# The tail of a one-core transformer block in another order: all of W1 for the first half of the last block before the last exp, the first part of Wo taken forward, and a second g buffer

## The chip, the core and the metric

The kernel runs on one core of a Trainium2 chip. A core has a matrix engine (TensorE, PE in the profile; PEld are its weight loads), a vector engine (VectorE, DVE), a scalar engine for table functions (ScalarE, ACT), a general engine (GpSimd, POOL) and a queue that issues transfers (SyncE, SP). Each works through its own list of instructions in order and waits on semaphores for the others. The metric is the device time of one execution in microseconds; three timed executions of the kernel before gave 780.62, 780.99 (the median) and 781.88.

## The reference

One transformer block with adaptive layer norm, on x of 2048 tokens by 512 channels, 32 heads of 16 channels, and a hidden layer of 1376:

```
mod = (silu(c) @ w_mod) split in six: sa, ca, ga, sb, cb, gb
h   = layernorm(x) * (1 + ca) + sa
q, k, v = h @ wqkv, per head
p   = softmax(q k^T * Dh ** -0.5)
x   = x + ga * ((p v) @ wo)
h   = layernorm(x) * (1 + cb) + sb
out = x + gb * (gelu(h @ w1 + b1) @ w2 + b2)
```

Weights and activations are bfloat16, sums are float32, GELU is the tanh form.

## The kernel before

**Tiling.** Queries are cut into 4 blocks of 512 tokens (`QB`), keys into 16 tiles of 128. A run is one query block with 4 heads, whose channels lie in four groups of 32 rows; there are 32 runs. In the last block a run holds 8 heads and 256 queries instead (`run_heads`), so that after half of its runs the first 256 of the last 512 tokens are complete. One unit is a score product of one head group with one key tile: a 32-row matmul of 512 columns (L803).

**Exps.** Scores go to PSUM tiles of three and two banks in turn (`st`, one buffer each), and ACT takes the exp of a whole tile (L852, `pt`). Some key tiles (`DKS`, 4 of 16) are done by DVE instead: scores in a one-bank tile (`ax`, two buffers) are turned into the bits of an approximate exponential (L900), and four shifted copies of them (L932, L953 on DVE; parts of the last one, L938, on POOL) are summed by the product with V. L994 is that product, on four column groups at once; it also sums the denominators.

**After a run** (`normalise`) DVE copies the result (L1019); SP moves the denominators through DRAM in small transfers (L1025, L1027), DVE takes their reciprocal (L1030), SP brings them back as a full tile (L1035, L1040), POOL multiplies (L1046) and SP moves rows to their place (L1056).

**After a block** (`block_tail`): the product with Wo (L1151), the sum with x (L1200), layer norm (`layer_norm`, statistics on DVE, the inverse root as an addition and a power on POOL, L604 and L606), transposes on PE (L672) and the scale and shift (`modulate`, L618 on DVE, L615 on ACT), W1 (L1217), the addition of b1 while leaving PSUM (L1227), one GELU over the block (L1236, with a table load before and after it), W2 (L1157), the last sum (L1248), and the transfer out. Wo and W2 hold the gates ga and gb, multiplied in by POOL early (L1069). In the last block `block_tail` runs for its first 256 tokens (`part`): W1 of the first 8 of 11 groups f of 128 hidden channels goes through DVE before the last exp, the other three (`direct`) after it, from the score banks that have come free (`r_t`, tiles `t`), with GELU straight from PSUM (L1223).

**The last 256 tokens** (`last_half`) are two tiles, t = 2 and 3. For each: transpose, reciprocal, transpose back and product on DVE (L1283, L1285, L1287, L1290), the two parts of Wo (L1151, L1297), sum (L1301), statistics, power, z (L610), transposes (L1317), modulation, W1 (L1329), GELU (L1332), W2, last sum (L1344).

**Order.** All engines' lists are written by a planner in the kernel (`Plan`), which runs through the operations with assumed durations and latencies. At each step it picks on each engine the ready operation with the lowest value of `dyn` (for PE) or `prio`, with a random scatter whose seed comes from `SEEDS`, one for each 12.5 us of planned time. `due` spreads a block's tail over a number of units (`TAIL`, `TAIL2`, `TAIL3`); kinds in `urgent` get 0.5, a second score tile in advance 2.2, P·V 3.0. The plan keeps a count of recent PE activity (`done`), and where this is low it puts in warming products on zeros (L430, L446, `heat`). The modulation columns (`mod_mm`, L575) are products of one output column, with a warming product after each second group (L578).

The lines that the planned order hangs on, in `dyn`:

```
        if o.kind == "qkA":
            back = n_a[0] - n_a[1]
            return (0.0 if back == 0 else 2.2 if back == 1 else 6.0) + same
...
        if o.kind in urgent:
            return 0.5 + same
        if o.kind == "last":
            return o.prio + 0.1 * same
```

## Time and profile before

| what | value |
|---|---|
| median of three timed executions | 780.99 us |
| the profiled execution, its own time | 779.58 us |
| its span, first to last instruction | 777.8 us |
| ACT busy | 750.5 us (96%) |
| PE busy | 722.0 us (93%) |
| DVE busy | 712.7 us (92%) |
| POOL busy | 281.2 us (36%) |
| mean granted TensorE clock | 0.995 |
| end of the last exp | 754.84 us |

The profile is that of one execution, and its span is shorter than its time by what lies around the program. A busy share is an average over stages: nearly all of the span is the attention, in which ACT is hardly ever idle, and the last 23 us are the tail of the last 256 tokens, in which it is idle half of the time. What counts for the end is therefore when ACT gets through its exps, and how long the chain behind the last one takes. Rows of a timeline give the start in the span, the duration, engine, line and operation, the tile written and read, and how often in a row; in brackets the idle time before it and what ended this.

### The profile page before, as it was taken

What the parts mean: (1) busy time and instruction counts of PE and PEld (TensorE: products, weight loads), DVE (VectorE), ACT (ScalarE), POOL (GpSimd) and SP (SyncE); (2) the same over time, 40 slices, a digit from 0 to 9 for tenths busy, and PEclk for the clock granted to TensorE, in tenths of its full rate; (3) what the DMA queues carried; (4) which work ended last, traced back from release to release, by engine and by line L of the source; (5) the groups of instructions that cost most, each with busy time, mean ns of one, the idle gap of its engine ahead of it and who ended that gap; (6) DMA issues with size and microseconds to landing.
All of it is one profiled execution on the core that took longest, in us unless ns stands there. A gap on an engine that the chain in (4) does not pass through costs nothing.

```text
span 777.8 us, 20624 instructions
## 1 busy us (share of the span) xinstructions
PE 722.0 (93%) x8233; PEld 274.2 (35%) x8307; DVE 712.7 (92%) x1180; ACT 750.5 (96%) x680; POOL 281.2 (36%) x622
## 2 busy tenths in 40 slices
PE   8888999999999889999998999999999999989998
PEld 3433333233333232323332323223234444434455
DVE  6777999999899999999999989999989998999964
ACT  3999999999999999999999999999999999999994
POOL 5221433444533334454444433333322423233320
PEclk9999998999999999999999999999999999999999
DMA  7033011000011010000100010000111000100010
GB/s 217 28 107 124 16 27 43 12 24 13 22 43 54 23 47 23 19 6 22 44 20 21 15 35 16 26 23 16 39 48 29 22 22 16 46 25 18 25 46 28
DMA packets 39074, 28.23 MB, mean 36 GB/s; under 512 B 17957, under 2 KB 34374, under 8 KB 38978
## 3 DMA queue, kind: packets, MB, share of 16 engines
q1 hardware_dynamic: 38970, 26.91, 12.1%
q8 instruction: 65, 1.06, 0.6%
q14 instruction: 31, 0.25, 0.1%
q10 hardware_dynamic: 8, 0.00, 0.0%
HBM read 21.30 MB, written 2.61 MB: 31 GB/s over the span
## 4 chain that ended last, share of the span: by engine, by line
ACT 50%; PE 27%; DVE 12%; issue 9%; DMA 1%; POOL 0%; SPq 0%; ACTq 0%; DVEq 0%; POOLq 0%
ACT pt L852 46%; PE od L994 9%; PE st L803 8%; DVE ph L900 5%; PE ax L1157 3%; DVE sh L953 2%; ACT g L1236 2%; PE ax L803 2%; DVE ph L953 1%; PE ax L693 1%; DMA blk<-in_w_mod_dram 1%; DVE sl L932 1%; DVE g L1227 1%; PE ax L1217 1%; PE t L1157 1%
## 5 line engine op out<-in xcount | busy, mean ns | idle before, releaser
L852 ACT ACTIVATE pt<-st 128x1536 bf16<-128x1536 f32 x626 | 708.6, 1408 | 4.4 <-PE st L803 2.3
L900 DVE TENSOR_SCALAR ph<-ax 128x512 int16<-128x512 f32 x484 | 318.1, 682 | 25.2 <-PE ax L803 22.3
L938 POOL TENSOR_TENSOR sl<-ph,step 128x128 int32<-128x128 int32 x358 | 163.7, 459 | 327.3 <-DVE sh L953 105.3
L803 PE MATMUL st<-qm,kT 32*128 32x512 bf16 x1564 | 245.7, 384 | 32.5 <-ACT pt L852 25.0
L803 PEld LDWEIGHTS <-kT 32*128 32x128 bf16 x2048 | 86.6, 91 | 244.1 <-issue 232.5
L803 PE MATMUL ax<-qm,kT 32*128 32x512 bf16 x484 | 162.5, 381 | 3.5 <-DVE ph L900 2.8
L994 PEld LDWEIGHTS <-VEB 128*32 128x32 bf16 x4992 | 109.6, 96 | 150.2 <-issue 128.0
L994 PE MATMUL od<-pt,VEB 128*32 128x512 bf16 (+1 forms) x1952 | 150.8, 344 | 0.9 <-ACT pt L852 0.5
L953 DVE TENSOR_SCALAR sh<-ph 128x4096 int16<-128x4096 int16 x121 | 146.9, 1217 | 2.5 <-PE od L994 2.2
L994 PE MATMUL od<-ph,VEB 128*32 128x512 bf16 (+1 forms) x1216 | 90.1, 340 | 1.7 <-DVE OD L1019 1.0
L994 PE MATMUL od<-sh,VEB 128*32 128x512 bf16 (+1 forms) x1216 | 84.6, 340 | 1.6 <-DVE sh L953 0.8
L953 DVE TENSOR_SCALAR ph<-ph 128x2048 int16<-128x2048 int16 x121 | 83.0, 687 | 0.4
L932 DVE TENSOR_SCALAR sl<-ph 128x1024 int16<-128x1024 int16 (+3 forms) x121 | 57.7, 482 | 0.4 <-PE od L994 0.4
L1046 POOL TENSOR_TENSOR OT<-OD,RB 128x128 bf16<-128x128 f32 x76 | 35.4, 470 | 48.1 <-DVE sh L953 14.8
L994 PE MATMUL od<-sl,VEB 128*32 128x512 bf16 (+1 forms) x608 | 48.4, 342 | 0.3
L1217 PE MATMUL ax<-blk,W 128*128 128x512 bf16 (+1 forms) x142 | 39.2, 358 | 2.0 <-issue 0.8
L1046 POOL TENSOR_TENSOR OS<-OD,RB 128x128 bf16<-128x128 f32 x48 | 22.8, 476 | 39.4 <-DVE sl L932 15.6
L693 PE MATMUL ax<-blk,w 128*128 128x512 bf16 x100 | 33.4, 383 | 3.3 <-ACT blk L615 1.7
L1227 DVE TENSOR_SCALAR g<-ax,b1c 128x512 bf16<-128x512 f32 (+1 forms) x41 | 28.0, 691 | 3.9 <-PE ax L1217 3.0
L1157 PE MATMUL ax<-w,g 128*128 128x512 bf16 x101 | 28.9, 381 | 1.1 <-DVE ph L900 0.6
L599 DVE BATCH_NORM_STATS2 ln_s<-xb 128x6 f32<-128x512 bf16 x32 | 21.6, 676 | 1.4 <-DMA xb<-in_A_x_dram 1.3
L1157 PEld LDWEIGHTS <-g 128*128 128x128 bf16 x176 | 13.7, 97 | 22.5 <-issue 12.8
(112 smaller groups left out, 400.8 us busy)
## 6 DMA issues: line engine op xcount, KB each, us to landing
RB<-rn SPq DMA_DIRECT2D x124, 64.0 KB
xb<-in_A_x_dram SPq DMA_DIRECT2D x8, 512.0 KB
out_dram<-o SPq DMA_DIRECT2D x16, 128.0 KB
qm<-qs SPq DMA_DIRECT2D x120, 16.0 KB
W<-in_B_w_dram SPq DMA_DIRECT2D x1, 1376.0 KB
w<-in_A_wqkv_dram SPq DMA_DIRECT2D x3, 384.0 KB
blk<-in_w_mod_dram SPq DMA_DIRECT2D x2, 512.0 KB
g<-in_w_mod_dram SPq DMA_DIRECT2D x2, 512.0 KB
```

The source lines that it names most:

```text
L693: return chain([(lambda ps, j=j: nc.tensor.matmul(out=ps[:, 0:QB], lhsT=w.tile[:, j, cc * P:(cc + 1) * P], rhs=o_h[b].tile[:, j, :], start ...
L803: nc.tensor.matmul(out=o.tile[:, k * QB:(k + 1) * QB], lhsT=kT[cc][kb][rows, ko * P:(ko + 1) * P], rhs=qm.tile[rows, par, :] if hb is None ...
L852: nc.scalar.activation(out=e.tile[:, 0:len(got) * QB], in_=o.tile[:, 0:len(got) * QB], func=ACT.Exp, scale=ESC)
L900: nc.vector.tensor_scalar(out=ph.tile[:, c0:c0 + QB], in0=o.tile, scalar1=PH_B, scalar2=0.0, op0=ALU.add, op1=ALU.max)
L932: parts = [in_turn(op("DVE", lambda o: nc.vector.tensor_scalar(out=into.tile[:, 0:cols], in0=first.tile[:, 0:cols], scalar1=PH_SH[-1], sca ...
L938: after_dve(nc.gpsimd.tensor_tensor(out=into.tile[:, c].bitcast(I32), in0=first.tile[:, c].bitcast(I32), in1=step, op=ALU.add))
L953: o = op("DVE", lambda o: nc.vector.tensor_scalar(out=dst(o), in0=src(), scalar1=PH_SH[j], scalar2=None, op0=ALU.add), us, deps, lat=DL, p ...
L994: nc.tensor.matmul(out=o_od[r].tile[32 * i:32 * i + 32, n * HB:n * HB + w], lhsT=v_tile(kt)[:, c0:c0 + 32], rhs=got[i][:, at:at + w], star ...
L1046: two = beside(lambda c: nc.gpsimd.tensor_tensor(out=OT.tile[:, c], in0=OD.tile[:, c], in1=o5.tile[:, c], op=ALU.mult), (OT,), (OD, o5))
L1157: nc.tensor.matmul(out=ps, lhsT=g[:, f, col:col + P], rhs=rhs, start=(f == 0), stop=(f == NF - 1))
L1217: mm = chain([(lambda ps, f=f, j=j: nc.tensor.matmul(out=ps[:, 0:N], lhsT=W1[:, j, f * P:(f + 1) * P], rhs=h.tile[:, j, 0:N], start=(j == ...
L1227: ev.append(op("DVE", lambda o, f=f, mm=mm: nc.vector.tensor_scalar(out=g.tile[:, f, 0:N], in0=mm.tile[:, 0:N], scalar1=b1c[:, f:f + 1], s ...
```

## The change

The first 256 tokens of the last block get a g buffer of their own (`r_gp`), so that all 11 groups of W1 go through DVE into it before the last exp, and the `direct` way through the score banks goes. GELU over that buffer is cut in four (`GE`) and comes after the last exp as before. The kind of this work becomes `late`, which is in `urgent`. The new buffer also holds the two broadcast gates until they are multiplied into the weights, in place of two constant tiles. `early_wo` takes the load of x for the last tiles and the first three products of Wo out of `last_half`; it is called when the next to last run has ended. In `last_half` the two tiles have a transposed buffer each, the second tile's DVE chain has other priorities and gates, the addition of EPS moves from POOL to DVE (L1316 of the changed kernel), and the transposes of tile 3 use the `ax` banks. W2 of the first half uses `r_t` banks, and its last sums wait for the second tile's z. The plan counts the modulation columns with less PE activity (`act`). `TAIL2` and `TAIL3` get smaller, and all values of `SEEDS` but the first are other ones (that line is left out below).

```diff
...
-        self.kb, self.due, self.extra = 0, 1e9, False
+        self.kb, self.due, self.extra, self.act = 0, 1e9, False, None
...
-            self.done.append((s, (o.us if o.mode[0] != "qk" else o.us * (len(o.mode) - 1) / 4)))
+            self.done.append((s, o.act if o.act is not None else (o.us if o.mode[0] != "qk" else o.us * (len(o.mode) - 1) / 4)))
...
+    LD = 0.11
...
-    PSUM_F = 8
...
+    r_gp = res("gp", 1, [P, NF, QB // 2], BF16)
...
-    urgent = set()
+    urgent = {"late"}
...
-            return (2.5 if o.due + 16 > prog() else 0.8) + same
+            return (2.5 if o.due + 16 > prog() else 0.8 if o.due + 48 > prog() else 0.3) + same
...
     TAIL, CB = 185, 49
-    TAIL2, TAIL3 = 148, 95
+    TAIL2, TAIL3 = 100, 60
     plan = Plan(dyn, later)
...
-        for n, (fn, us) in enumerate(pieces):
+        for n, (fn, us, *act) in enumerate(pieces):
...
+            o.act = act[0] if act else None
...
-    ga_bc = const.tile([P, D], FP32, name="ga_bc")
-    gb_bc = const.tile([P, D], FP32, name="gb_bc")
...
     def mod_columns(dst, ws, kind, warmer=True):
-        mm = chain([(lambda ps, n=n, w=w, m=m: mod_mm(ps, n, w[1](), m, warmer), 0.36 if warmer else 0.22)
+        mm = chain([(lambda ps, n=n, w=w, m=m: mod_mm(ps, n, w[1](), m, warmer), 0.36 if warmer else 0.22, 0.17 * (m % 2) + 0.01)
                     for n, w in enumerate(ws) for m in range(NC)],
...
             got += beside(lambda c, w=w: nc.gpsimd.tensor_tensor(
-                out=w()[:, c], in0=w()[:, c], in1=gate_t[:, c], op=ALU.mult), deps, prio=2.0)
+                out=w()[:, c], in0=w()[:, c], in1=gate_t()[:, c], op=ALU.mult), deps, prio=2.0, rel=(o_late["gates"],))
         return op("NIL", None, 0.0, got, lat=0.0, prio=0.0)
+
+    def gate_tile(n):
+        return lambda: o_late["gates"].tile.rearrange("p f q -> p (f q)")[
+            :, 2 * D * n:2 * D * (n + 1)].bitcast(FP32)
...
         return scaled([lambda f=f: W2[f // 4].tile[:, f % 4, :] if f < 8 else W2c[:, f - 8, :] for f in range(NF)],
-                      gb_bc, (W2[0], W2[1], o_late["small"], o_late["gb"]))
+                      gate_tile(1), (W2[0], W2[1], o_late["small"], o_late["gb"]))
...
             stop=(j == NC - 1)), MM) for j in range(NC)], [s], kind, r_ax, (s, w))
-        return op("DVE", lambda o: nc.vector.tensor_copy(out=dst, in_=mm.tile), 0.66, (mm,),
+        return op("DVE", lambda o: nc.vector.tensor_copy(out=dst(), in_=mm.tile), 0.66, (mm, o_late["gates"]),
                   prio=0.1, rel=(mm,))
...
     def block_tail(b, nt=TPB):
-        kind = "tail"
+        kind = "tail" if b < LAST else "late"
         due(prog() + 15, (TAIL if b < LAST - 1 else TAIL2 if b < LAST else TAIL3) / (9 * nt - 1))
...
                                     None, r_blk, ("DVE",) * 4, r_ax, kind, 0.3, None, nt)
-        g = op("NIL", None, 0.0, hd, lat=0.0, prio=0.0, acq=r_g)
         part = nt < TPB
+        g = op("NIL", None, 0.0, hd, lat=0.0, prio=0.0, acq=r_gp if part else r_g)
         if part:
-            g.uses += 1
-            o_late["part"] = g
             one = ones(g, (g,))
         ev = []
-        over = op("NIL", None, 0.0, (), lat=0.0, prio=0.0, gate=finished) if part else None
         if part:
...
         for f in range(NF):
-            direct = part and f >= PSUM_F
             mm = chain([(lambda ps, f=f, j=j: nc.tensor.matmul(
...
                 start=(j == 0), stop=(j == NC - 1)), nt * MM / NC) for j in range(NC)],
-                hd + [o_late["w1"], g, over if direct else None], kind,
-                r_t if direct else r_ax, (h,))
-            if direct:
-                ev.append(op("ACT", lambda o, f=f, mm=mm: nc.scalar.activation(
-                    out=g.tile[0:rows(f), f, 0:N], in_=mm.tile[0:rows(f), 0:N], func=ACT.Gelu_apprx_tanh,
-                    bias=b1c[0:rows(f), f:f + 1], scale=1.0), 0.36, (mm,), lat=0.15, prio=0.4, rel=(mm,)))
-                continue
+                hd + [o_late["w1"], g], kind, r_ax, (h,))
             ev.append(op("DVE", lambda o, f=f, mm=mm: nc.vector.tensor_scalar(
...
                 op0=ALU.add), 0.13 + nt * 0.134, (mm, o_late["b1"]), prio=0.3 if part else 0.1, rel=(mm,)))
+        GE = ((0, 2), (2, 5), (5, 8), (8, NF))
         if part:
...
                 0.2 * (hi - lo) * nt / 2 + 0.1 + 1.3 * (lo == 0), ev[lo:hi], lat=0.15, prio=0.5,
-                gate=finished) for lo, hi in ((0, 2), (2, PSUM_F))]
+                gate=finished) for lo, hi in GE]
+            o_late["ev"] = ev
         else:
...
             mm = chain([(lambda ps, t=t, f=f: w2_mm(ps, g.tile, t * P, f, f + 1), MM)
-                        for f in range(NF)], (prev, one, o_late["w2"]), "part" if part else kind, r_ax, (g,), 3,
-                       lambda f: ge[0] if not part else ge[f >= 2] if f < PSUM_F else ev[f])
+                        for f in range(NF)], (prev, one, o_late["w2"]), "part" if part else kind, r_t if part else r_ax, (g,), 3,
+                       lambda f: ge[sum(f >= hi for _, hi in GE)] if part else ge[0])
             prev = mm
...
                 out=o.tile, in0=mm.tile, in1=x2.tile[:, t, :], op=ALU.add), 0.6,
-                (mm,), prio=3.0 if part else 0.1, acq=r_o, rel=(mm, x2))
+                (mm,), prio=3.0 if part else 0.1, acq=r_o, rel=(mm, x2),
+                gate=(lambda: "norm" in o_late and o_late["norm"][-1].end is not None) if part else None)
             dma(lambda o, t=t, a=a: nc.sync.dma_start(
...
                 rel=(a,))
+            if not part:
+                o_late.setdefault("outs", []).append(a)
         due(1e9)
+
+    def early_wo():
+        b = LAST
+        o_late["xr"] = load_x(b)
+
+        def ready():
+            return not own[NR - 1] and not shared[NR - 1] and all(e.end is not None for e in o_late["ev"] + o_late["outs"])
+        acc = {t: op("NIL", None, 0.0, (), lat=0.0, prio=2.0, acq=r_ax, gate=ready) for t in (2, 3)}
+        o_late["acc"] = acc, {t: op("PE", lambda o, t=t: wo_mm(acc[t].tile, b, t, 0, 3), 3 * MM,
+                                    [acc[t]] + [x for u in range(NC, 7) for x in o_OT[(b, u)].two], lat=PEL,
+                                    mode=("full", 0), kind="last", prio=0.5) for t in (2, 3)}
...
         full = ("full", 0)
-        xr = load_x(b)
+        xr = o_late["xr"]
...
         ln, z, h = take(r_ln, (x2,)), take(r_z, (x2,)), take(r_blk, (x2,))
-        g = o_late["part"]
-        od, OD, OT = o_od[r], take(r_OD), take(r_OT)
+        g = take(r_g)
+        one = ones(g, (g,))
+        od, OT, ODs = o_od[r], take(r_OT), [take(r_OD), take(r_OD)]
         o_OT[(b, 7)] = OT
         tiles = (2, 3)
-        acc = {t: take(r_t) for t in tiles}
-        early = {t: op("PE", lambda o, t=t: wo_mm(acc[t].tile, b, t, 0, 3), 3 * MM,
-                       [acc[t]] + [x for u in range(NC, 7) for x in o_OT[(b, u)].two], lat=PEL, mode=full,
-                       kind="last", prio=0.5) for t in tiles}
-        s = None
+        acc, early = o_late["acc"]
+        mul, stat = [None, None], [None, None]
+        norm = []
         for n, t in enumerate(tiles):
+            OD = ODs[n]
             den = work.tile([P, 8], FP32, name=f"den{t}")
...
-            def turned(n):
+            def turned(n, OD=OD):
                 return OD.tile[:, n * HB:(n + 1) * HB].rearrange("p (a q) -> p a q", a=2)
-            sh = op("DVE", lambda o, t=t, half=half: nc.vector.transpose(out=turned(0), in_=half(od.tile)), 0.35,
-                    (o_last[r], OD, s), prio=0.06 + n)
-            rc = op("DVE", lambda o, den=den: nc.vector.reciprocal(
-                out=den, in_=OD.tile[:, 16:HB:32]), 0.12, (sh,), prio=0.05 + n)
-            bk = op("DVE", lambda o, den=den: nc.vector.transpose(
+            sh = op("DVE", lambda o, half=half, turned=turned: nc.vector.transpose(out=turned(0), in_=half(od.tile)), 0.45,
+                    (o_last[r], OD), lat=LD, prio=(0.01, 0.03)[n], gate=(None, lambda: mul[0].end is not None)[n])
+            rc = op("DVE", lambda o, den=den, OD=OD: nc.vector.reciprocal(
+                out=den, in_=OD.tile[:, 16:HB:32]), 0.2, (sh,), lat=LD, prio=(0.009, 0.0295)[n])
+            bk = op("DVE", lambda o, den=den, turned=turned: nc.vector.transpose(
                 out=turned(1).rearrange("p a q -> p (a q)"),
-                in_=den.unsqueeze(2).to_broadcast([P, 8, 32])), 0.35, (rc,), prio=0.045 + n)
-            ml = [op("DVE", lambda o, t=t, half=half: nc.vector.tensor_tensor(
+                in_=den.unsqueeze(2).to_broadcast([P, 8, 32])), 0.45, (rc,), lat=LD, prio=(0.008, 0.029)[n],
+                    gate=(None, lambda: stat[0].end is not None)[n])
+            ml = [op("DVE", lambda o, half=half, turned=turned: nc.vector.tensor_tensor(
                 out=half(OT.tile), in0=half(od.tile), in1=turned(1), op=ALU.mult),
-                0.36, (bk, OT), prio=0.04 + n)]
+                0.36, (bk, OT), prio=(0.007, 0.0125)[n])]
+            mul[n] = ml[0]
...
                 out=x2.tile[:, t, :], in0=acc[t].tile, in1=xr.tile[:, t, :], op=ALU.add), 0.62,
-                (w, x2, xr), prio=0.024 + n / 50, rel=(acc[t],))
-            s = op("DVE", lambda o, t=t: stats(ln, t, x2.tile[:, t, :]), 0.83, (a, ln), prio=0.022 + n / 50)
-            rs = op("POOL", lambda o, t=t: rstd(ln, t, t + 1), 0.9, (s,), prio=0.0)
+                (w, x2, xr), lat=LD, prio=(0.012, 0.016)[n], rel=(acc[t],))
+            s = op("DVE", lambda o, t=t: (stats(ln, t, x2.tile[:, t, :]), nc.vector.tensor_scalar(
+                out=ln.tile[0][:, t, 1:2], in0=ln.tile[0][:, t, 1:2], scalar1=EPS, scalar2=None, op0=ALU.add)), 0.95, (a, ln), lat=DPL, prio=(0.014, 0.02)[n])
+            stat[n] = s
+            rs = op("POOL", lambda o, t=t: nc.gpsimd.tensor_tensor(
+                out=ln.tile[1][:, t:t + 1], in0=ln.tile[0][:, t, 1:2], in1=mhalf[:, 0:1], op=ALU.pow), 0.7, (s,), prio=0.0)
             za = op("DVE", lambda o, t=t: apply(ln, z, t, x2.tile[:, t, :]), 0.33, (rs, z),
-                    prio=0.021 + n / 50)
+                    prio=(0.011, 0.013)[n])
+            norm.append(za)
+            o_late["norm"] = norm
...
                                             in_=z.tile[:, t, j * P:(j + 1) * P], identity=ident)
-                tro = op("PE", tr, 2 * 0.0705, (za,), lat=PEL, mode=full, kind="last", acq=r_t, prio=0.1)
-                for n, j in enumerate(js):
-                    hd.append(op(e, lambda o, n=n, j=j, e=e, at=at, tro=tro: modulate(
+                tro = op("PE", tr, 2 * 0.0705, (za,), lat=PEL, mode=full, kind="last", acq=(r_t, r_ax)[n], prio=0.1)
+                for m, j in enumerate(js):
+                    hd.append(op(e, lambda o, n=m, j=j, e=e, at=at, tro=tro: modulate(
                         e, h.tile[:, j, at], tro.ps[:, n * P:(n + 1) * P], modB, j), 0.25, (tro, h),
-                        prio=0.02, rel=(tro,)))
-            gs = slice(HB + (t - 2) * P, HB + (t - 1) * P)
+                        prio=(0.015, 0.0145)[n], rel=(tro,)))
+            gs = slice((t - 2) * P, (t - 1) * P)
             gd = []
...
                     w2_mm((first_of[id(o)] or o).tile, g.tile, gs.start, f, f + 1)
-                o = op("PE", w2, MM, (gd[f], prev), lat=PEL if f == NF - 1 else 0.0, mode=full,
+                o = op("PE", w2, MM, (gd[f], prev, one), lat=PEL if f == NF - 1 else 0.0, mode=full,
                        kind="last", acq=r_t if f == 0 else None, prio=0.4)
...
                 late_loads(o_last[0])
-                o_late["ga"] = gate_bc(ga_bc, o_late[2], "gate")
+                o_late["gates"] = op("NIL", None, 0.0, (), lat=0.0, prio=0.0, acq=r_gp)
+                o_late["gates"].uses += 1
+                o_late["ga"] = gate_bc(gate_tile(0), o_late[2], "gate")
                 o_late["wo"] = scaled([lambda u=u: Wo[:, u, :] for u in range(NC)] +
-                                      [lambda p=p: WoP[:, p, :] for p in range(2)], ga_bc,
+                                      [lambda p=p: WoP[:, p, :] for p in range(2)], gate_tile(0),
                                       (o_late["wo"], o_late["ga"]))
...
                 o_late[5] = load_w(wm_src[:, :, 5 * D:6 * D], r_xb, (o_late["ga"],), prio=5.0)
-                o_late["gb"] = gate_bc(gb_bc, o_late[5], "gate")
+                o_late["gb"] = gate_bc(gate_tile(1), o_late[5], "gate")
                 urgent.add("gate")
...
                 o_late["w2"] = w2_scaled()
+                o_late["gates"].uses -= 1
                 state["w2"] = True
...
                 block_tail(b, 2)
+            if r == NR - 2:
+                early_wo()
             if r == NR - 1:
```

2 lines of the change are left out of this document (1 added, 1 removed).

## The prediction

> **What bounds the kernel now.** I read the page first (shares, chain), then the busy time by stretches, then the timelines around ScalarE's idle places and behind the last exp.
>
> ```profile
> span 777.8 us, 20624 instructions
> ...
> ACT 50%; PE 27%; DVE 12%; issue 9%; DMA 1%; POOL 0%; SPq 0%; ACTq 0%; DVEq 0%; POOLq 0%
> ...
> L852 ACT ACTIVATE pt<-st 128x1536 bf16<-128x1536 f32 x626 | 708.6, 1408 | 4.4 <-PE st L803 2.3
> ```
>
> ScalarE (ACT) computes 626 exps and leads the chain. The stretches show where it idles:
>
> ```profile
> core 0: us, PE busy (x) PEld busy (x) DVE busy (x) ACT busy (x) POOL busy (x), PEclk, DMA share, GB/s
> ...
> 16.00:45.00 29.00, 23.91 (x226) 11.34 (x228) 20.56 (x50) 26.86 (x28) 5.66 (x12) 1.00 0.18 57
> 45.00:132.00 87.00, 79.51 (x858) 28.82 (x861) 78.80 (x129) 87.00 (x79) 30.97 (x67) 1.00 0.22 64
> 132.00:140.00 8.00, 7.68 (x68) 2.00 (x67) 6.18 (x15) 6.68 (x7) 2.61 (x6) 0.57 0.09 28
> 140.00:600.00 460.00, 432.32 (x4537) 145.37 (x4583) 445.52 (x708) 459.79 (x401) 178.09 (x389) 1.00 0.10 27
> 600.00:625.00 25.00, 23.72 (x381) 10.51 (x379) 24.36 (x45) 24.69 (x22) 9.41 (x20) 1.00 0.10 27
> 625.00:754.84 129.84, 121.92 (x1918) 57.55 (x1931) 118.04 (x192) 129.71 (x113) 42.34 (x91) 1.00 0.09 25
> 754.84:777.80 22.96, 19.01 (x164) 12.03 (x166) 10.43 (x24) 11.80 (x32) 1.60 (x4) 0.99 0.14 47
> ```
>
> Read length minus ACT busy: 2.14 us idle in 16 to 45, none in 45 to 132, 1.32 in 132 to 140, 0.21 in 140 to 600, 0.31 in 600 to 625, 0.13 up to the last exp's end at 754.84. So up to there only some 4.1 us could be won, all but 0.65 of it before 140. After it comes a tail of 22.96 us in which TensorE (PE) is busy 19.01. Two of the idle places, and the tail:
>
> ```profile
> 43.53 0.39 PE L803 MATMUL st<-qm,kT 32*128 32x512 bf16 x2 [0.37 <-ACT kT L623]
> ...
> 44.02 3.28 ACT L852 ACTIVATE pt<-st 128x1024 bf16<-128x1024 f32 x3 [0.54 <-PE ax L803]
> ```
> ```profile
> 134.98 3.28 ACT L852 ACTIVATE pt<-st 128x1024 bf16<-128x1024 f32 x3 [0.45 <-PE ax L803]
> 139.13 2.37 ACT L852 ACTIVATE pt<-st 128x1536 bf16<-128x1536 f32 x2 [0.87 <-PE ax L803]
> ```
> ```profile
> 754.84 1.28 ACT L1231 ACT_TABLE_LOAD   x1
> ...
> 756.13 0.63 ACT L1231 ACTIVATE g<-g 128x512 bf16<-128x512 bf16 x1
> ...
> 757.02 1.47 ACT L1231 ACTIVATE g<-g 128x1536 bf16<-128x1536 bf16 x1
> 757.03 0.31 PEld L1297 LDWEIGHTS <-OT 128*128 128x128 bf16 x2
> 757.25 0.59 PE L1297 MATMUL t<-WoP,OT 128*128 128x512 bf16 x2
> ...
> 757.94 0.69 DVE L1301 TENSOR_TENSOR xb<-t,xb 128x512 bf16<-128x512 f32 x1 [1.03 <-PE t L1297]
> ...
> 766.55 2.80 PE L1329 MATMUL t<-blk,W 128*128 128x128 bf16 x44
> ...
> 774.35 0.69 DVE L1248 TENSOR_TENSOR o<-ax,xb 128x512 bf16<-128x512 f32 x1 [0.33 <-PE ax L1157]
> ```
>
> In brackets stands the idle time before a row and what ended it. PE works from 755.17 (its first W1 matmul behind the last exp) to 774.31 almost without a gap; the last sum ends at 775.04 and the span 2.76 later.
>
> **The change, part by part.** Sums are against the profiled execution: 779.58 us, span 777.8 and 1.78 around it; the median shown, 780.99, is 1.41 above it. The number and shapes of exps, GELU and table-load places before the tail are the same, so ACT's own work up to the last exp is unchanged, and only its idle time can move.
>
> 1. The modulation columns (L575, products of one output column) are now booked in the plan as 0.01 or 0.18 us of PE activity rather than 0.36. In 132.7 to 139.5 the granted clock was 0.55 on average; the 512-column matmuls there took 512 to 634 ns against 381 to 385 after it, and ACT idled 0.45 + 0.87. Just ahead, at 129.3 to 131.8, three groups of these columns stand with only scores and small warming products between them. In the changed order one group of 8 columns at most stands between two score tiles and 4 to 16 P·V products of full width follow each. Counting each order by score tile (a product by its columns, a quarter for a 32-row one, nothing for a one-column one), the emptiest 3.4 us of the old order past the first is 0.30 busy and lies there; in the new order it is 0.36, and the old order has 0.36 in two other places where the clock stayed at 1.00. I take the whole 1.32 as gone; ends 0 and -1.32.
> The Trainium skill ("TensorE: Matmul & The Clock Gate", Part 1) says that the clock falls to half after an idle window of about 3.4 us, and that this window runs freely and does not start with the kernel. The fall to half for 6.8 us agrees. By its second half the fall need not be in every execution, and then less is won in the median: that is the second rival.
>
> 2. Start. The 0.54 at 44.02 stands behind a K product (3 of its 4 matmuls there, 1.04 us) and 12 V products (0.83 us) in one gap between scores, then the copy of K on ACT. In the new order K is split over the two gaps before, and only 4 V products stand before the first score on that key block. I take -0.54; ends 0 and -0.54. The first 20 us are the same order, and its waits (1.11 and 0.48 behind the layer norm of block 1) stay.
>
> 3. The new start values of the scatter (SEEDS) and the shorter due spans (TAIL2 148 to 100, TAIL3 95 to 60) reorder everything from 22 us on. That this order stalls ACT elsewhere the trace of before cannot show. From below: no new stall, and the old 0.31 gone; from above: the 2.14 us of 29 that the start shows, once more. I take 0, nearest the row of 140 to 600 (0.21 in 460 us under the same planner).
>
> 4. W1 before the last exp: 12 matmuls of 256 columns (0.94 for 7: (0.94 - 0.27)/6 = 0.111 each, 1.33 us) leave the tail, and 3 more evictions on VectorE (DVE, 0.48 each) go before it. Between the last three score issues of the new order stand 7 and 8 W1 matmuls: 0.78 and 0.89 plus 0.32 for each score issue, 2.3 us against 1.33 + 0.91 of exps. DVE has its last shift out by then, and in the old order idles 2.43 us there. So I take 0, ends 0 and +0.5.
>
> 5. The tail, walked in the new order from the same 754.84 (L1309 and L1313 are lines of the changed kernel). The six Wo products are first now, 755.17 to 756.46 (0.2155 each; 0.39 for one, 0.17 of it drain). ACT: table 1.28, then GELU of f 0-1 until 756.75 and, since 512 columns take 0.63 and 1536 take 1.47, 0.84 for 768 columns: f 2-4 until 757.49, then 758.23 and 758.97. PE's queue holds W2 of f 0, 1 and 2 ahead of the second part of Wo (L1309), so this waits for the second GELU: it starts at 757.87 and not 757.25, though OT is ready at 756.86. The sum (L1313) is at 758.55 to 759.24, statistics 0.69 + 0.18, the new EPS addition 0.16 to 0.20 on DVE (0.155 for the 128x1 rows at L537), POOL's power 0.57 instead of 0.23 + 0.57; but DVE now also has the second transpose and product of tile 3 (0.45 + 0.42) before z, which ends at 761.77 (760.99 before). The second Wo part of tile 3 ends at 762.13, its sum at 762.90, and only then does DVE modulate tile 2: 763.51 (762.42 before). W1 of tile 2 starts at 763.63 (762.55), on three banks. z of tile 3 ends at 765.77 (765.39); an output sum (0.68) precedes its modulation, 767.09 (766.44). ACT is done with its two at 767.1, four GELU of tile 2 follow, and W1 of tile 3 starts at 767.44 when the first of them frees its bank, for 44 x 0.06 = 2.64, to 770.09. Then 22 W2 products, 4.74: 774.83, with the drain 775.00. Last sum to 775.7, plus 2.76: 778.45, or +0.6. Cross-check by PE's sum: all its work in the tail is 17.4 us (18.7 before), but its gaps grow from 0.24 to some 2.2: -1.33 + 1.96. Ends: no gap at all, -1.57; gaps half again as long, +1.7.
>
> 6. Costed at nothing: the gate tile in the new g buffer (its 68 scalings keep their count and their engine), and the memset of ones on POOL, which works 1.60 us in the old tail. The load of x for the last tiles, one 0.58 us issue and 512 KB, moves on SP's queue from behind the last normalised run's transfers (issued at 753.60) to ahead of that run's first one (L1025, old 735.97). Behind it wait this transfer, the next, and the reciprocal of the denominators, which stands in DVE's order with two shifts and two evictions behind it. In the old order the second transfer was issued at 737.71 and the reciprocal came only at 742.24, 4.5 us later, which hides the issue and most of the 512 KB. If the cover is gone DVE waits: I take 0, ends 0 and +1.0. In exchange the load no longer lands in the tail, where it kept nobody.
>
> Sum: -1.32 - 0.54 + 0 + 0 + 0.6 = -1.26. Profiled 778.3; median 780.99 - 1.26 = 779.7.
>
> **The rivals.** First, the tail does get shorter: if PE's queue is not held behind the second GELU and the gaps come to 1 us, the tail is -1.33 + 0.76 = -0.57 instead of +0.6, and the median 778.5. For it: 12 matmuls really leave a stretch that PE fills without a gap. Against: the order of PE and DVE above. Second, the half clock stays, or comes elsewhere, or was not in the median runs: -1.26 + 1.32, 781.05. For it: 0.36 is not far from 0.30. Third, slower: the work of the last block's first half is now "late", with priority 0.5 against 2.2 for a second score tile in advance, and block 2's tail is pressed into two thirds of its span. Each chain of 4 W matmuls of 512 columns (0.86) in front of a three-bank score issue, whose cover is the 0.91 of the two-bank exp less 0.49 from score to exp (43.53 to 44.02), costs 0.44. It decides from 7 such places on (1.56 + 1.26 over 0.44); with 8 the median is 783.2. Against: the old plan let the same chains pass with 0.13 idle in 129.84 us.
>
> **How the numbers follow.** 0.2% is 1.56 us, about what this measurement can tell from no change: the borders are 779.43 and 782.55. The forecast (779.7, own range 778.9 to 780.5) has 0.52, of which 0.25 below 779.43 and 0.27 within; the shorter tail 0.17, all faster; the half clock 0.11, all within; the slower case 0.20. Faster 0.42, same 0.38, slower 0.20. From 777.9 (the shorter tail with the 0.31 gone also) to 782.8 about 0.8 is held; beyond lie the fuller stalls and a tail without gaps.
>
> **What would show it.** Right: granted clock 1.00 throughout, ACT idle 1.7 to 2.2 us between its first and last exp, last exp's end near 753.0, tail near 23.6, PE's first L1309 about 3.0 us behind the last exp's end (2.4 before), W1 of tile 3 starting 12.6 behind it (11.7). Wrong: new idle places of ACT between 140 and the last exp, a second stretch at half clock, or a tail under 22.5.

## The result, and the profile after

The changed kernel takes 777.93 us in the median of 22 executions (776.52 to 782.71); the kernel before takes 780.69 us in 22 beside them. The ratio is 0.9972, 95% interval 0.9961 to 0.9984: faster by 2.2 us (1.2 to 3.0; the medians differ by 2.8), as forecast in sign, and below the forecast value of 779.7 us. A second set of 12 executions gave 777.85 us, ratio 0.9975 (0.9958 to 0.9992).

To read a profile here one has to know that executions of one and the same kernel differ by 6 to 7 us, mostly by how long TensorE's granted clock stands at half. The profiled execution of the changed kernel was a long one, 780.45 us, that of before a short one, 779.58 us. Set side by side, these two would make the change a loss. Its busy times by stretch, with the columns of the table shown for before:

```profile
core 0: us, PE busy (x) PEld busy (x) DVE busy (x) ACT busy (x) POOL busy (x), PEclk, DMA share, GB/s
16.00:45.00 29.00, 24.77 (x228) 11.22 (x227) 21.79 (x51) 27.93 (x29) 5.75 (x12) 1.00 0.23 73
132.00:140.00 8.00, 7.55 (x81) 2.40 (x79) 6.50 (x12) 8.00 (x8) 4.51 (x10) 1.00 0.02 3
140.00:420.00 280.00, 262.15 (x2724) 87.13 (x2720) 275.93 (x445) 279.68 (x245) 118.17 (x260) 1.00 0.10 27
420.00:436.00 16.00, 15.66 (x112) 3.56 (x109) 12.32 (x21) 13.07 (x11) 5.35 (x11) 0.57 0.02 6
600.00:625.00 25.00, 22.66 (x401) 10.73 (x398) 24.56 (x43) 24.54 (x22) 7.79 (x15) 1.00 0.08 21
755.88:778.70 22.82, 18.85 (x161) 10.74 (x159) 10.94 (x27) 11.58 (x31) 1.10 (x2) 1.00 0.07 24
```

The half clock at 132 to 140 is gone: PEclk 1.00 where it was 0.57, ACT busy 8.00 of 8.00. Another stands at 420 to 436 (0.57), where before had none, and ACT idles 2.93 us there. ACT's idle time in 16 to 45 fell from 2.14 to 1.07 us. The last stretch, from the last exp's end, is 22.82 us long (22.96 before). The timeline of ACT in the two changed places, idle time and what ended it in brackets; first the copy of K near 25 us before the change, then the changed kernel:

```profile
25.12 0.59 ACT L623 CAST kT<-ax 128x512 bf16<-128x512 f32 x1 [1.11 <-PE ax L693]
```
```profile
24.01 0.59 ACT L623 CAST kT<-ax 128x512 bf16<-128x512 f32 x1 [0.46 <-PE ax L693]
...
40.77 6.12 ACT L852 ACTIVATE pt<-st 128x1536 bf16<-128x1536 f32 x5
...
424.85 2.53 ACT L852 ACTIVATE pt<-st 128x1536 bf16<-128x1536 f32 x2 [0.55 <-PE st L803]
428.37 2.53 ACT L852 ACTIVATE pt<-st 128x1536 bf16<-128x1536 f32 x2 [0.99 <-PE st L803]
431.54 2.37 ACT L852 ACTIVATE pt<-st 128x1536 bf16<-128x1536 f32 x2 [0.64 <-PE st L803]
```

The exp that waited 0.54 us for K's copy at 44.02 has no wait any more. The copy before it waits 0.46 us (1.11 before): DVE now modulates the block behind one pair of statistics rows, where it had two pairs ahead of it. At half clock every pair of exps waits for its scores. The tail, behind the last exp's end at 755.88:

```profile
758.82 0.59 PE L1309 MATMUL ax<-WoP,OT 128*128 128x512 bf16 x2
...
764.11 2.06 PE L1346 MATMUL t<-blk,W 128*128 128x128 bf16 x28
...
767.68 2.67 PE L1346 MATMUL t<-blk,W 128*128 128x128 bf16 x44 [0.26 <-ACT g L1349]
...
775.23 0.69 DVE L1361 TENSOR_TENSOR o<-t,xb 128x512 bf16<-128x512 f32 x1 [1.68 <-PE t L1161]
```

The second Wo part starts 2.94 us behind the last exp (forecast 3.0), W1 of tile 2 8.23 (8.79), W1 of tile 3 11.80 (12.6).

### The profile page after: what moved, and what is told of

It is laid out like the page before. It is cut to its first block, busy times and chain, and to the rows that moved or that the text cites. A ratio compares the mean times of both kernels' runs of the same rounds, so it can differ in the third digit from the quotient of the medians.

```text
span 778.7 us, 20637 instructions
## 1 busy us (share of the span) xinstructions
PE 729.6 (94%) x8281; PEld 273.5 (35%) x8281; DVE 715.2 (92%) x1185; ACT 751.0 (96%) x679; POOL 279.4 (36%) x619
## 4 chain that ended last, share of the span: by engine, by line
ACT 53%; PE 24%; DVE 12%; issue 9%; DMA 1%; POOL 0%; SPq 0%; DVEq 0%; ACTq 0%
ACT pt L852 52%; PE od L994 8%; PE st L803 7%; DVE ph L900 5%; PE ax L1217 2%; DVE sh L953 2%; PE ax L1161 2%; DVE ph L953 1%; PE t L1161 1%; PE ax L803 1%; PE ax L693 1%; DMA blk<-in_w_mod_dram 1%; DVE xb L1204 1%; PE t L1346 1%; ACT g L1232 1%
## 5 line engine op out<-in xcount | busy, mean ns | idle before, releaser
L900 DVE TENSOR_SCALAR ph<-ax 128x512 int16<-128x512 f32 x484 | 318.4, 684 | 23.6 <-PE ax L803 18.8
L994 PE MATMUL od<-pt,VEB 128*32 128x512 bf16 (+1 forms) x1952 | 149.0, 344 | 0.4 <-DVE OD L1019 0.2
L1217 PE MATMUL ax<-blk,W 128*128 128x512 bf16 (+1 forms) x176 | 43.3, 355 | 0.3 <-DVE ph L900 0.2
L693 PE MATMUL ax<-blk,w 128*128 128x512 bf16 x124 | 36.4, 385 | 2.0 <-DVE blk L618 1.1
L1221 DVE TENSOR_SCALAR g<-ax,b1c 128x512 bf16<-128x512 f32 x33 | 24.4, 743 | 3.9 <-PE ax L1217 3.8
L1161 PE MATMUL ax<-w,g 128*128 128x512 bf16 x96 | 26.4, 382 | 0.6 <-DVE ph L900 0.5
L1019 DVE COPY OD<-od 128x512 f32<-128x512 f32 x31 | 21.2, 683 | 0.8 <-PE od L994 0.8
```

The costliest lines, as they stand in the source:

```text
L693: return chain([(lambda ps, j=j: nc.tensor.matmul(out=ps[:, 0:QB], lhsT=w.tile[:, j, cc * P:(cc + 1) * P], rhs=o_h[b].tile[:, j, :], start ...
L900: nc.vector.tensor_scalar(out=ph.tile[:, c0:c0 + QB], in0=o.tile, scalar1=PH_B, scalar2=0.0, op0=ALU.add, op1=ALU.max)
L994: nc.tensor.matmul(out=o_od[r].tile[32 * i:32 * i + 32, n * HB:n * HB + w], lhsT=v_tile(kt)[:, c0:c0 + 32], rhs=got[i][:, at:at + w], star ...
L1161: nc.tensor.matmul(out=ps, lhsT=g[:, f, col:col + P], rhs=rhs, start=(f == 0), stop=(f == NF - 1))
L1217: mm = chain([(lambda ps, f=f, j=j: nc.tensor.matmul(out=ps[:, 0:N], lhsT=W1[:, j, f * P:(f + 1) * P], rhs=h.tile[:, j, 0:N], start=(j == ...
L1221: ev.append(op("DVE", lambda o, f=f, mm=mm: nc.vector.tensor_scalar(out=g.tile[:, f, 0:N], in0=mm.tile[:, 0:N], scalar1=b1c[:, f:f + 1], s ...
```

## The experiments

The theory at the start was the prediction's: half clock behind the modulation columns taken away in every execution (1.3 us), the wait for K's copy taken away (0.5), and the tail a little longer (+0.6) because the new order of its chains eats the moved products. The rivals: the half clock comes and goes by chance and the change only alters how often; the tail is shorter; the new start values of the scatter alone make the gain.

### How often each kernel runs at half clock

No edit: both kernels again, for the mean clock of each execution.

> The kernel before, unchanged, for the granted clock of each of its executions. The prediction's reading (the half clock at 132.7 to 139.5 stands in the order of the work, and the change takes it away for 1.32 us in every execution): at least 8 in 10 executions show a mean clock near 0.991 (6.83 of 778 us at half), and the few without it are some 1.3 us shorter. The rival (the same order falls to half clock in some executions and not in others, and the change only alters how often): between 3 and 8 in 10 executions at 0.99, the others at 0.998 to 1.00, with 1.3 us or more between the two groups.

> The changed kernel, unchanged, for the granted clock of each execution. The prediction's reading: clock 1.00 in nearly all executions, time 2 to 3 us below the kernel before. The rival of chance: a quarter to a third of its executions show 0.99 and are 2 to 4 us longer (a half clock of two windows in 420 to 436 costs 2.8 us of ScalarE's idle time), and those without it stand only some 1.0 to 1.5 us below those executions of the kernel before that have none.

The first expectation holds a slip: 6.83 us of 778 at half make a mean clock of 0.9956, not 0.991. In the traces every half-clock stretch but the last measured 3.4, 6.8 or 13.7 us, whole multiples of about 3.41 us ("windows" below); the last is a piece at the very end, of which 1.3 us at most lie in the span. So a clock of 0.999 or more is no window, 0.997 or 0.998 is one, 0.995 or 0.996 two, 0.993 three, 0.991 or less four or more. All executions of the two kernels with a listed clock, by windows at half clock (number, median us):

| windows | before, 91 executions | changed, 34 executions |
|---|---|---|
| 0 | 6, 778.04 | 12, 776.99 |
| 1 | none | 12, 777.93 |
| 2 | 22, 779.04 | none |
| 3 | 36, 780.67 | 5, 780.46 |
| 4 and more | 27, 781.92 | 5, 780.66 |

85 of 91 executions of before have two windows or more, 10 of 34 of the changed kernel. So chance is part of it, but a small part: the order of the work decides, as the prediction had it. A straight line through the executions gives 0.99 us for each window in either kernel. The mean count fell from 3.26 windows to 1.52, at that price 1.73 us of the 2.16 by which the means differ (780.61 and 778.45). But the price depends on the place: by ACT's idle time a window costs 0.66 us at the columns (1.32 for two) and 0.73 at 420 (2.93 for four), against 1.2 and 1.5 in two places shown further down, and the executions of before with two windows are 1.0 us longer in the median than those with none. So the two at the columns are worth 1.0 to 1.3 us. The second expectation counts two windows at 420; there are four.

Without any window the changed kernel is still 1.05 us shorter (776.99 against 778.04). An execution without one was caught in the second set (776.95 us, span 775.2), called the undisturbed one below:

```profile
16.00:45.00 29.00, 24.57 (x227) 11.22 (x227) 21.76 (x52) 27.93 (x29) 5.75 (x12) 1.00 0.21 67
132.00:140.00 8.00, 7.55 (x80) 2.38 (x78) 6.47 (x12) 8.00 (x8) 4.35 (x10) 1.00 0.01 2
420.00:436.00 16.00, 14.40 (x143) 4.89 (x142) 15.21 (x25) 16.00 (x15) 8.41 (x16) 1.00 0.05 10
600.00:625.00 25.00, 22.56 (x404) 10.93 (x394) 24.52 (x44) 24.54 (x23) 6.34 (x14) 1.00 0.09 22
752.39:775.20 22.81, 18.85 (x161) 10.74 (x159) 10.94 (x27) 11.58 (x31) 1.10 (x2) 0.98 0.07 24
```

Same instructions, same order, and the stretch 420 to 436 is at full clock with ACT busy throughout. Its first exp starts 0.49 us earlier than in the profile of before, although the instructions up to there stand in the same order:

```profile
15.79 6.88 ACT L852 ACTIVATE pt<-st 128x1536 bf16<-128x1536 f32 x6 [1.52 <-PE st L803]
```
```profile
15.30 2.37 ACT L852 ACTIVATE pt<-st 128x1536 bf16<-128x1536 f32 x2 [1.52 <-PE st L803]
```

The upper row is before, the lower one the undisturbed execution, read over a shorter stretch. So some of the 1.05 us can be the start, which varies between executions of one order; how much is open.

### Where the other windows of before are

> The kernel before once more, for one more profiled execution: where an execution at a clock of 0.993 or less (three half windows of 3.41 us or more) has those beyond the two at 132.7 to 139.5. If the start carries the third: a half window inside 8 to 45 and ScalarE idling some 1.0 us more there. If another place in the middle does: a half window between 140 and 750. At 0.995 it shows the two at 132.7 alone once more.

> As the run ahead of it, a further execution of the kernel before: the same two theories for the third half window (start, or between 140 and 750), and the two at 132.7 to 139.5 in it as well if the order of the modulation columns is their cause.

The first look, a 782.20 us execution (stretches at the start, at the modulation columns, and behind the GELU of a later block):

```profile
10.50:14.00 3.50, 3.28 (x17) 1.69 (x16) 1.54 (x3) 1.45 (x2) 1.17 (x4) 0.56 0.94 285
132.00:140.00 8.00, 7.52 (x70) 2.21 (x71) 6.55 (x14) 7.02 (x7) 2.61 (x6) 0.61 0.11 36
684.00:700.00 16.00, 13.88 (x166) 6.25 (x168) 13.93 (x26) 14.78 (x11) 5.76 (x12) 0.89 0.10 29
```

The second look, 780.13 us:

```profile
10.50:14.00 3.50, 3.02 (x25) 1.60 (x24) 1.49 (x4) 1.52 (x3) 1.17 (x4) 1.00 0.97 291
132.00:140.00 8.00, 7.52 (x67) 2.02 (x66) 6.21 (x14) 6.72 (x7) 2.62 (x6) 0.57 0.13 32
684.00:700.00 16.00, 14.24 (x181) 6.22 (x184) 15.56 (x29) 15.96 (x11) 5.99 (x12) 1.00 0.10 29
```

All four profiles of before have the two windows at 132 to 140. The extra ones of the first look are one in the start, which moved its first exp to 16.60 (15.79, 15.78 and 16.03 in the other three), and one behind the GELU at 685, where an exp then waits 1.17 us for its scores. So both theories for the third window are right in part: it comes in the start and behind a GELU.

### Warming the modulation columns alone

In the kernel before, a warming product behind every product group of the columns:

```
-        if m % 2 and warmer:
+        if warmer:
```

> The kernel before with 4 more warming products of 384 columns, one behind every product of a modulation column where it had one behind every second; order otherwise the same, whole reference computed. If the emptiness of TensorE around the modulation columns (128 to 132) is what halves the clock: no half clock at 132 to 140 in any execution, mean clock 0.998 or more in nearly all, and the executions that would have had it are 1.3 us shorter, so a median 0.5 to 1.3 us below the kernel before; ScalarE idles nothing in 132 to 140. If the half clock has another cause there, or comes from execution to execution anywhere: the same share of executions at 0.99 as the kernel before and the same time within 0.3 us.

Median 779.73 us against 780.38 beside it, ratio 0.9997 (0.9983 to 1.0011). The place itself answered: first line below. Ten of its 12 executions have at most two windows (two have three), where before has three or more in 63 of 91. But two other things stand in its profile, one window in 16 to 45 (clock 0.94) and ACT idle 1.03 us in 600 to 625 (0.31 before):

```profile
132.00:140.00 8.00, 7.42 (x94) 2.70 (x97) 7.66 (x17) 8.00 (x9) 3.08 (x7) 1.00 0.09 28
600.00:625.00 25.00, 23.21 (x355) 9.95 (x351) 23.38 (x44) 23.97 (x22) 9.24 (x19) 1.00 0.09 25
```
```profile
601.11 0.25 DVE L1030 RECIPROCAL dc<-dc 128x16 f32<-128x16 f32 x1 [1.19 <-DMA dc<-dn]
```

There DVE stood 1.19 us for the transfer of the denominators, and three exps behind it waited 0.27, 0.28 and 0.17 us. Its five executions at a clock of 1.00 fall apart into 777.38 and 777.49 against 779.34, 779.51 and 779.53. So the emptiness around the columns causes the half clock there: that is shown. The time won by it could not be told from nothing in this run, because some 2 us that are no half clock came and went. That they are the late transfer is argued, not shown. Its profiled execution is not one of the five.

### The start values alone, and everything but them

Only the line SEEDS exchanged, in the kernel before and back in the changed one.

> The kernel before with only the start values (SEEDS) of the changed kernel; the dependencies and the tail are those of the kernel before. If the new start values alone carry what is gained ahead of the tail: half clock at the modulation columns gone, the 0.54 us wait for the copy of K at 44 gone, last exp's end about 1.9 us earlier than in the kernel before's profile (754.84), tail unchanged at 22.96, time 778.5 to 779.5. If the start values only suit the other edits (the booking, the spans, the new tiles change what is drawn): the modulation columns stand as badly as before or elsewhere, and the time is anywhere between 779 and 783, with ScalarE idle places that neither kernel has.

> The changed kernel with the start values (SEEDS) of the kernel before, all other edits kept. If the start values belong to the order that they were drawn for (the new ones made the kernel before 22 us slower): 790 to 810 us, ScalarE idle 10 to 25 us between its first and last exp, tail within 1 of 22.8. If the other edits carry the gain and the start values only add: 778 to 781.

802.24 us (ratio 1.0280, 1.0253 to 1.0308) and 813.47 us (1.0414, 1.0389 to 1.0438). Both lie outside every range that was expected. The new values in the kernel before, two stretches, its exps, then its ACT waits (us in total, times, longest; the first of them is in the tail):

```profile
16.00:45.00 29.00, 25.76 (x220) 11.44 (x219) 20.30 (x49) 26.55 (x28) 5.76 (x12) 0.88 0.16 46
140.00:600.00 460.00, 430.52 (x4326) 140.88 (x4319) 411.22 (x654) 447.92 (x389) 175.67 (x384) 0.99 0.09 26
```
```profile
L852 ACT ACTIVATE pt<-st 128x1536 bf16<-128x1536 f32 x635 | 720.5, 1395 | 10.6 <-PE ax L803 4.3
```
```profile
ACT blk L615 <- PE t L1317: 4.9, 2, 4.2
ACT L1236 <- DVE g L1227: 4.4, 1, 4.4
ACT pt L852 <- PE ax L803: 4.3, 3, 3.2
ACT pt L852 <- PE st L803: 4.1, 6, 1.5
```

ACT idles 12.08 us in 140 to 600, where it idled 0.21, 4.4 of it ahead of one block GELU whose inputs DVE has late. About as much is not waiting but work: ACT takes 635 exps for 720.5 us, where the kernel before takes 626 for 708.6, because the plan leaves DVE fewer score products to turn into exponentials (460 rows of L900 in place of 484). The changed kernel with the old values, which has 640 exps and 448 rows:

```profile
140.00:600.00 460.00, 422.77 (x4237) 138.10 (x4278) 410.62 (x650) 453.91 (x395) 163.71 (x360) 0.99 0.09 26
600.00:785.44 185.44, 170.85 (x2644) 78.45 (x2648) 161.21 (x265) 178.99 (x155) 59.64 (x121) 0.98 0.09 26
785.44:811.60 26.16, 20.28 (x154) 11.23 (x155) 10.55 (x26) 11.58 (x31) 1.10 (x2) 0.93 0.07 22
```

Here ACT idles 6.09 and 6.45 us, and the tail is 26.16 us long. Neither half of the change gives a faster kernel by itself. The scatter is computed from the start value and from an operation's number in the list (`o.seq`), so edits that add or take operations draw anew; each of the two exchanges was 22 or 33 us slower. Both orders are at full clock at 132 to 140. So the expectation that the new values carry the gain falls, and so does the other, that the edits carry it without them. How much of the 2.2 us is the edits and how much a well drawn order is not separated by any run here, and no line of the diff can be named that gives it.

### The moved W1 products, put back as empty work

```
...
+            if t == 2:
+                for k in range(12):
+                    nc.tensor.matmul(out=bank(4)[:, 0:2 * P], lhsT=W1[:, k % 4, (8 + k // 4) * P:(9 + k // 4) * P],
+                                     rhs=W1[:, 0, 0:2 * P], start=(k % 4 == 0), stop=(k % 4 == 3))
             wo_mm(acc[t].tile, b, t, 0, 3)
```

> The changed kernel with 12 extra products of 256 columns (0.111 us each, 1.33 us together) between the last product of the last probabilities and the first Wo products of the tail: TensorE does again in the tail what the change moved out of it (their results go into a bank that is overwritten, so the whole reference is still computed). Tail 22.82 us in the changed kernel. If TensorE's work sets the tail: tail 24.1. If the chain through the second Wo part sets it (prediction's step 5): the products fill the 0.42 and 0.62 us of waits ahead of that part first, it starts 0.8 to 0.9 later, tail 23.6. If the moved products did not matter: tail 22.8.

The tail is 23.64 us (last exp's end 752.86, span 776.5), median 779.31 us (10 executions):

```profile
756.70 0.59 PE L1315 MATMUL ax<-WoP,OT 128*128 128x512 bf16 x2
...
761.98 2.06 PE L1352 MATMUL t<-blk,W 128*128 128x128 bf16 x28
...
765.56 2.67 PE L1352 MATMUL t<-blk,W 128*128 128x128 bf16 x44 [0.26 <-ACT g L1355]
```

Second Wo part at 3.84 us behind the last exp (2.94 without the products), W1 of the tiles at 9.12 (8.23) and 12.70 (11.80): all of it 0.9 later. This is the middle expectation, 23.6. The 12 products of 1.33 us cost 0.82 in the tail, the rest went into waits for GELU.

### The order of the tail

The second Wo part ahead of the W2 product that waits for the second GELU:

```
-                0.2 * (hi - lo) * nt / 2 + 0.1 + 1.3 * (lo == 0), ev[lo:hi], lat=0.15, prio=0.5,
+                0.2 * (hi - lo) * nt / 2 + 0.1 + 1.3 * (lo == 0), ev[lo:hi], lat=0.65 if lo == 2 else 0.15, prio=0.5,
...
+            o_late["pw2"] = mm
...
-                mm = op("PE", w1, 4 * 0.071, hd, lat=PEL, mode=full, kind="last", acq=r_t, prio=0.3)
+                mm = op("PE", w1, 4 * 0.071, hd + [o_late["pw2"]], lat=PEL, mode=full, kind="last", acq=r_t, prio=0.3)
```

The last two lines keep W1 of the tiles behind W2 of the first half, where it stands in the changed kernel.

> The changed kernel with the second Wo part of the first last tile ahead of the W2 product that waits for the second GELU, not behind it (one latency of the plan raised; W1 of that tile has 24 products instead of 28 ahead of the other tile's transposes). Prediction's step 5 says this wait holds the chain: the second Wo part then starts 2.5 us behind the last exp instead of 2.94, W1 of the first last tile 7.8 instead of 8.2, and the tail is 0.3 to 0.45 shorter, 22.4. If the tail's end hangs on the other tile's chain (its z, its W1 behind ScalarE's GELUs): the same tail within 0.15.

Tail 22.53 us (755.57 to the span's 778.1), 0.29 shorter:

```profile
758.00 0.60 PE L1310 MATMUL ax<-WoP,OT 128*128 128x512 bf16 x2
...
763.51 1.75 PE L1347 MATMUL t<-blk,W 128*128 128x128 bf16 x24
...
766.87 2.92 PE L1347 MATMUL t<-blk,W 128*128 128x128 bf16 x48 [0.26 <-ACT g L1350]
```

The Wo part starts at 2.43 us, W1 of tile 2 at 7.94, of tile 3 at 11.30. The wait was the one that the prediction named, and the chain through it sets the end. The median, 778.10 us (12 executions, 4 of them at three windows or more), is not below that of the changed kernel.

And DVE's two chains as before the change, W1 still ahead of the last exp (the priorities, and two gates, of the tiles' DVE work from the first transpose to the modulation; two of eight are shown, and W1 behind W2 is kept as above):

```
-                    (o_last[r], OD), lat=LD, prio=0.06 + n, gate=(None, lambda: stat[0].end is not None)[n])
+                    (o_last[r], OD), lat=LD, prio=(0.01, 0.03)[n], gate=(None, lambda: mul[0].end is not None)[n])
...
-                0.36, (bk, OT), prio=0.04 + n)]
+                0.36, (bk, OT), prio=(0.007, 0.0125)[n])]
```

> The changed kernel with the order of DVE's two chains in the tail as before the change (the other tile's shift, product and sum come behind the first tile's statistics, and its second Wo part behind the W2 products), W1 still ahead of the last exp. If the new order of the chains costs what the prediction's step 5 gave it (gaps of 2.2 us against 0.24): the old order with 1.33 us less of TensorE's work gives a tail of 21.6 to 22.3. If the new order is what makes use of the moved products: W1 of the second tile starts later than 11.8 us behind the last exp and the tail is 23.0 to 23.6.

Tail 22.92 us (752.08 to 775.0), between the two expectations: 0.10 more than the changed kernel and 0.04 less than before.

```profile
755.01 0.59 PE L1309 MATMUL ax<-WoP,OT 128*128 128x512 bf16 x2
...
760.50 3.16 PE L1346 MATMUL t<-blk,W 128*128 128x128 bf16 x44
...
764.76 2.80 PE L1346 MATMUL t<-blk,W 128*128 128x128 bf16 x44
```

W1 of tile 3 does start late (12.68 us), but four W2 products of tile 2 run ahead of it (1.03 us; one of their records is missing). So the order of the chains hardly matters while W1 is out of the tail. The median is 778.12 us (10 executions).

### Filling the gap behind the GELU

Seven products of zeros, added onto running sums of Wo and Q in the place ahead of the half clock at 420:

```
...
+            n_wo[0] += 1
+            if n_wo[0] in (30, 31, 32):
+                zero(ps)
...
+            for _ in range({105: 3, 106: 1}.get(n_pr[0], 0)):
+                zero(ps[:, 0:QB])
```

> The changed kernel with 7 products of zeros (512 columns, 0.2155 us each, added onto running sums, so nothing computed changes) between the Wo and Q products behind the first block's GELU, where TensorE had 1.21 us idle (417.9 to 419.15) right ahead of the half clock at 420.4 to 434.1 of the changed kernel's profiled execution; all else in the same order. If that emptiness sets off the half clock of the changed kernel: at most 1 or 2 in 10 executions at a clock of 0.993 or less instead of 10 in 34, the median 777.0 to 777.6 and no execution above 780. If the half clock of the changed kernel has other places too, or comes without such a gap: still about 3 in 10 at 0.993 or less, median 777.9.

> The changed kernel with both earlier edits: the 7 products of zeros behind the first block's GELU, and the second Wo part of the first last tile ahead of the W2 product that waits for the second GELU. If both effects are as measured and add up: tail 22.5 (22.82 in the changed kernel), at most 2 in 12 executions at a clock of 0.995 or less, their median 777.4 to 777.8. If the products of zeros only move the half clock to other places: a quarter or more at 0.995 or less and a median of 777.9 or more.

Alone: 778.11 us, one execution in 12 at three windows (780.45 us) and one at two, so the expected share, but neither the expected median nor a highest time below 780. With the Wo edit: 778.52 us (8 executions), two at two windows, tail 22.55 us. Its profile has a window in another place, at 600 to 625, where ACT idles 1.98 us (0.46 in the undisturbed execution):

```profile
600.00:625.00 25.00, 22.34 (x367) 10.86 (x364) 23.08 (x40) 23.02 (x21) 5.88 (x13) 0.93 0.08 19
```

Of the 20 executions with the filling one reached three windows; of the 66 of the other four kernels in the changed order (changed, dummy products, Wo ahead, old chains) 16 did. But only 4 of the 20 had no window, against 22 of the 66; 12 of the 20 had a single one, which lay in the start in the profile of the filling alone (clock 0.79 in 8 to 16). So the long half clock became rarer, short ones in other places more frequent, and the combined run came out as its second expectation has it (two of 8 at 0.995, median 778.52). That the gap sets off the half clock at 420 is pointed to, not shown: the numbers are too small, and the median did not move. The ratio to before is 0.9963 (0.9949 to 0.9976) with both edits, against 0.9972 (0.9961 to 0.9984) for the changed kernel: no version here is shown to beat it.

## Why the prediction was right, and by how much it was off

The sign was right, and the likeliest case (779.7, own range 778.9 to 780.5) was 1.8 us too high; 777.93 lies at the very edge of the range from 777.9 to 782.8. That it lies inside is luck: the lower end stands for the shorter tail with the old 0.31 gone, which is not what came and by the prediction's own numbers gives 778.2 (778.5 - 0.31), and the second set's 777.85 is outside. Point by point:

1. **Half clock at the columns, -1.32.** The place and its cause were right: two windows there in four of four profiles of before, none in any profile of the changed order, none with warming alone. The size holds for these two windows (1.0 to 1.3 us). It was read off one execution with two windows, while the commonest kind of before has three and the commonest of the changed kernel none or one; but if the 85 executions all have the two at the columns, before has some 1.4 windows elsewhere and the changed kernel 1.5, so the mean count fell by about the two. That the booking of the columns (`act`) does it was wrong: without that edit the planner writes the same instructions in the same order, so the booking does nothing here, and the columns came to stand differently with the rest of the redrawn order.
The Trainium skill ("TensorE: Matmul & The Clock Gate", Part 1) says that the window of about 3.4 us runs freely and that one kernel therefore warms differently from run to run; the stretches of 3.4, 6.8 and 13.7 us and the two profiles of one order, one with and one without the windows at 420, agree. The "idle" window that the prediction takes from there is not an empty one here: TensorE's longest pause ahead of the half clock was 1.21 us at 420 and 0.48 at the columns.

2. **Wait for K's copy, -0.54.** Right, in both profiles of the changed kernel. But the prediction left the 1.11 us at 25 as it was, arguing from the same order up to 20 us. The wait lies behind that, and DVE's new order there takes 0.65 off it. Another 0.12 us of idle time appears at 22, so ACT's idle time in 16 to 45 falls by 1.07.

3. **New start values, 0.** The new small stalls before the last exp: in the undisturbed execution ACT idles 0.18 more than before in 140 to 420, 0.15 more in 600 to 625 and 0.21 more from there to the last exp, together 0.54, within the ends of -0.31 and +2.14. The order drawn here was a good one: the two exchanges of start values cost 22 and 33 us, far outside those ends.

4. **W1 ahead of the last exp, 0.** Right: ACT idles 0.02 us from 740 to the last exp in either profile of the changed kernel.

5. **The tail, +0.6.** It measured -0.14, so this step failed in size and sign. The wait that it names held (the second Wo part behind the second GELU, at 2.94 against 3.0 forecast); the gaps behind it were mis-sized. Against before, the dummy products show the two sides: the new order with the same TensorE work costs 23.64 - 22.96 = +0.68, and the moved products give 0.82. The prediction had the gaps at 1.96 and the products at 1.33. The two sides do not simply add: with DVE's old order the moved products give only 0.04 (22.92 against 22.96). The walk loses step by step: counted from the last exp, the end of z of tile 2 was forecast at 6.93 us and measured at 6.54, W1 of tile 2 at 8.79 and 8.23, W1 of tile 3 at 12.60 and 11.80. From the end of tile 2's sum to the end of its z it has 2.53 us, where 2.28 were measured: it added some 0.03 between DVE's operations, while the transpose and z start 0.07 before the row ahead of them ends.

6. **Load of x and the rest, 0.** In none of the changed kernel's two profiles did DVE wait for the reciprocal's transfer. Right as far as seen.

With these sizes the terms are -1.32 - 0.54 - 0.65 + 0.12 + 0.54 - 0.14 = -1.99, near the difference of the means (-2.16). The 1.8 us by which the forecast was too high are 0.7 from the terms (mostly the tail, as the 0.65 and the 0.54 nearly cancel), 0.3 from the starting point (780.99 from three executions, 780.69 from 22) and some 0.8 from the medians, which differ by more than the terms (777.93 - 780.69 = -2.76), as the middle execution has three windows before the change and one behind it. Of the rivals, "the half clock comes elsewhere" took place in 10 of 34 executions and is what the slow end of the changed kernel consists of; "the tail is shorter" took place with a quarter of its size; no slower case came. The list of what would show it right asked for a clock of 1.00 throughout, and only 12 of 34 executions had that (0.999 or 1.000); one of its signs of being wrong, a second stretch at half clock, did come, in the profiled execution itself. And the step from the half clock to the time rests on ACT's idle time there and on the line through the executions: warming the columns alone took the half clock away, but no gain in time could be measured.

## What to carry to other kernels

Before a half-clock stretch in one profile is priced, the clocks of many executions should be laid out: the place, its frequency and its length are three numbers, and the price of a window differs from place to place. A walk through a tail that adds a small gap at every step ends some tenths too late; the rows of the same chain before the change show how large the gaps are. And where a scatter with drawn start values orders the work, an edit to the operations redraws it, so a change with new values can only be judged whole.

## What the runs showed of the hardware

- Half clock came in whole windows of some 3.41 us. On average each cost 0.99 us of the kernel's time, about the same in both kernels; by ACT's idle time it was 0.66 us at the modulation columns, 0.73 at 420, 1.2 at 685 and 1.5 at 600 to 625.
- The same list of instructions had none to six windows (a mean clock of 0.999 to 0.986): 6, 22, 36 and 27 of 91 executions of before had 0, 2, 3 and 4 or more. One place had them in every profile, others (the start, the stretches behind a GELU) now and then.
- In these kernels, whose first 20 us are the same order, the first exp started between 14.85 and 16.60 us behind the first instruction; the two latest (16.40 and 16.60) had a half-clock window in the start.
- The transfer of the denominators, which DVE met without a wait in the first profile of before, kept it 0.4 us in the second and 1.2 us in one place with the columns warmed.
